# Cosine attention into a leaky-relu MLP on one core: squares and two copies to ScalarE, one weight asked for in a row, two turnings a group later

## The chip, the cores and the metric

The kernel runs on 1 core of one Trainium2 chip. The metric is the device time of one execution in microseconds (us). Engines: TensorE (PE; its weight loads are the row PEld), VectorE (DVE), ScalarE (ACT), GpSimd (POOL) and SyncE (SP). DMAs are asked for on the queues of SP, ScalarE and GpSimd.

## The reference

```python
# q, k, v: (8, 12, 448, 64) f32; tau = 0.1; w_in: (768, 2048); w_out: (2048, 768)
q_n = q / (norm(q, axis=-1) + 1e-6)
k_n = k / (norm(k, axis=-1) + 1e-6)
scores = q_n @ k_n.T / tau
attn = softmax(scores)                    # over the keys
x = (attn @ v).transpose(0, 2, 1, 3).reshape(3584, 768)
h = x @ w_in
out = maximum(0.01 * h, h) @ w_out        # (3584, 768) f32
```

## The kernel before

The twelve heads of a batch are six **pairs** of heads. Pairs are numbered through, `s` from 0 to 47, so that pairs 0 to 5 are batch 0 and 6 to 11 batch 1. The "tenth pair" is `s = 9`. The 448 tokens of a head are three tiles of 128 and a remainder of 64.

What one pair passes through before TensorE can make its scores:

- `load_qk` or `load_pairs`: rows of q and k from DRAM into one of six places in `raw_sb`.
- `squares(s)`, line 173: two multiplications (512 and 384 elements a partition, f32), on GpSimd as a rule; for `nc.scalar` it is an activation with Square.
- `sums(s)`, line 186: two reductions on VectorE.
- `roots(s)`, line 197: Ln and Exp on ScalarE, for the square root.
- `normalise(s)`, line 213: on VectorE an addition (line 217), a reciprocal (218) and two scalings (222) that write `qn`.
- `transposes(s)`, line 248: for `s < 10` seven turnings on TensorE (line 236) into one PSUM bank and a copy into `qkT` (line 260); from 10 on a DMA.

`norm(s)` is roots, normalise, (turnings,) then `hold`, and the squares of a later pair. `hold(x)` (line 511) is a copy of one column on GpSimd: GpSimd's queue goes on only when `x` has been written. All engines run their queues in the order in which the program writes them; nothing reorders them.

Behind the scores stand `key_tiles` (TensorE's scores, ScalarE's Exp into `pe`, or `pr` for the remainders), `totals`, `products` and `scale`, which give `xT`. The MLP of a batch is `firsts` (16 groups m of six matmuls, each drained by ScalarE into `hT` by Prelu, lines 374 to 390) and `groups` or `second` (line 458 or 420, with `w_out_sb`). PSUM has eight banks, given out by age by `banks`.

The stage that the change touches begins at line 754: `attend(NQ - 1)` closes batch 0's attention. Then `firsts(0, ...)` runs batch 0's groups m, and between them, at the m given in a table, the last four pairs that TensorE turns are prepared: pairs 6 to 9. Behind m = 15 the first `visit` starts with `key_tiles([(7, 3), (9, 3)])`, the key remainders of pairs 6 and 7 and of 8 and 9. They need `qkT` of all four. In that stage GpSimd's queue holds, in order: `hold(xT)`, two quarters of `w_out` (line 111, 768 KB each), `hold(qn[6])`, the squares of pair 9, `hold(qn[7])`, a quarter of `w_out`, the squares of pair 10, `hold(qn[8])`, the last quarter, the squares of 11, then loads of v.

Of the kernel before, what the change touches and what calls it, by code (L numbers as in the profile page):

```python
# [16 lines left out]
def kernel(  # L17
# [10 lines left out]
    nc = tc.nc  # L28
# [12 lines left out]
    MT = D_ff // 128  # L41
# [67 lines left out]
    def load_w_out(parts):  # L109
        for m in parts:  # L110
            gp.dma_start(out=w_out_sb[:, m : m + MT // 4], in_=w_out_r[:, m : m + MT // 4])
# [25 lines left out]
    def load_qk(s):  # L137
        if s >= NSLOT:
            return
        b, h0 = s // NPAIR, 2 * (s % NPAIR)  # L140
        both = raw_sb[:, s % NPAIR]
        nc.sync.dma_start(out=both[:, :, 0:3], in_=main(q, b, h0, 2))
        nc.sync.dma_start(out=both[:, :, 4:7], in_=main(k, b, h0, 2))
        for i, x in enumerate((q, k)):
            nc.sync.dma_start(
                out=both[64 * i : 64 * i + 64, :, 3],
                in_=x[b, h0 : h0 + 2, MAIN:S].rearrange("h p d -> p h d"),
            )
        raw[s] = (both[:, :, 0:4], both[:, :, 4:7])
# [23 lines left out]
    def squares(s, engs=(gp, gp)):  # L173
        if s >= NSLOT:
            return
        tiles = []
        for x, eng, name in zip(raw[s], engs, ("sq0", "sq1")):
            sq = sqp.tile(list(x.shape), F32, name=name)
            if eng is nc.scalar:
                nc.scalar.activation(sq, x, func=AF.Square)  # L180
            else:
                eng.tensor_tensor(sq, x, x, op=ALU.mult)  # L182
            tiles.append(sq)
        sqs[s] = tiles

    def sums(s, parts=(0, 1)):
        if s >= NSLOT:
            return
        if s not in ss:
            ss[s] = smp.tile([128, 14], F32, name="ss")  # L190
        for i in parts:
            o = ss[s][:, 0:8] if i == 0 else ss[s][:, 8:14]
            nc.vector.tensor_reduce(  # L193
                o.rearrange("p (h t) -> p h t", h=2), sqs[s][i], axis=AX.X, op=ALU.add
            )

    def roots(s):
        if s >= NSLOT:
            return
        nc.scalar.activation(ss[s], ss[s], func=AF.Ln, bias=tiny)  # L200
        nc.scalar.activation(ss[s], ss[s], func=AF.Exp, scale=0.5)  # L201

    qn, scalings = {}, {}
# [9 lines left out]
    def normalise(s):  # L213
        if s >= NSLOT:
            return
        r = smp.tile([128, 14], F32, name="r")
        nc.vector.tensor_scalar_add(ss[s], ss[s], 1e-6)  # L217
        nc.vector.reciprocal(r, ss[s])  # L218
        qn[s] = qnp.tile([128, 7, 2, D], BF16, name="qn")
        for x, lo, hi, r0 in ((raw[s][0], 0, 4, 0), (raw[s][1], 4, 7, 8)):  # L220
            nt = hi - lo
            scalings[s] = nc.vector.tensor_tensor(  # L222
                qn[s][:, lo:hi],
                x.rearrange("p h t d -> p t h d"),
                r[:, r0 : r0 + 2 * nt].rearrange("p (h t) -> p t h", h=2)
                .unsqueeze(3).to_broadcast([128, nt, 2, D]),
                op=ALU.mult,
            )
# [5 lines left out]
    def one(tp, s, lo, hi):  # L234
        for t in range(lo, hi):
            nc.tensor.matmul(
                out=tp[:, t, :],
                lhsT=qn[s][:, t].rearrange("p h d -> p (h d)"),
                rhs=id128,
                is_transpose=True,  # L240
                start=(t == lo),
                stop=(t == hi - 1),
            )

    def transposed():
        return banks(1).bitcast(BF16)[:, : 7 * 128].rearrange("p (t c) -> p t c", c=128)

    def transposes(s):
        if s >= NSLOT:
            return  # L250
        dst = qtp.tile([128, 7, 128], BF16, name="qkT")
        qkT[s] = dst.rearrange("p t c -> p (t c)")
        if s >= DMA_FROM:
            nc.sync.dma_start(
                out=dst, in_=qn[s].rearrange("p t h d -> p (t h d)"), transpose=True
            )
            return
        tp = transposed()
        one(tp, s, 0, 7)
        nc.vector.tensor_copy(out=dst, in_=tp)  # L260

    pe, pr = {}, {}

# [247 lines left out]
    def hold(x):  # L511
        seen = smp.tile([128, 1], F32, name="seen")
        gp.tensor_copy(out=seen, in_=x)  # L513
# [28 lines left out]
    dst = qtp.tile([128, 7, 128], BF16, name="qkT")  # L542
    qkT[0] = dst.rearrange("p t c -> p (t c)")
    for lo, hi in ((0, 4), (4, 7)):
        tp = transposed()
# [45 lines left out]
    for s in range(2):  # L591
        scores(s, (0, 1))
        fill(2 if s else 5)
        scaled(s)
        scores(s, (2,))
        if s:
            fill(2)
            scores(s, (3,))
        transposes(s + 1)
        fill(2)  # L600
        roots(s + 2)
# [4 lines left out]
    scores(2, (2,))  # L606
    fill(2)
    transposes(3)
    roots(4)
    reciprocals(0)  # L610
# [6 lines left out]
    scores(3, (2,))  # L617
    fill(1)
    transposes(4)
    roots(5)  # L620
    scores(3, (3,))
# [66 lines left out]
    def attend_batch(b):  # L688
        if b == 1:
            load_qk(14)  # L690
            load_qk(15)
            sums(12)
        attend_two(b * NQ)
        if b == 1:
            norm(12)
        attend(b * NQ + 2)


    def norm(s, transposed=True):
        if s >= NSLOT:  # L700
            return
        roots(s)
        normalise(s)
        if transposed:
            transposes(s)
        if s == 10:
            return
        for x in (12, 13) if s == 11 else (s + 4,) if s > 11 else ():
            load_qk(x)
        hold(qn[s][:, 6, 0, 0:1])  # L710
        if s < 9:
            load_w_out((4 * (s - 5),))
        if s == 11:
            squares(12)
        if s != 9:
            squares(s + (3 if s < 9 else 2))

    def firsts(b, begun, between):

        for m in range(begun, AHEAD):  # L720
            pms[b, m] = banks(1, (b, m, 0))
            first(b, m, range(KT - 2))
        for m in range(MT):
            for fn in between.get(m, ()):
                fn()
            first(b, m, range(KT - 2 if m < max(begun, AHEAD) else 0, KT))
# [18 lines left out]
    def at(*steps):  # L745
# [8 lines left out]
    attend(NQ - 1, [lambda m=m: first(0, m, range(KT - 2)) for m in range(3, SOON)])  # L754
    normalise(6)
    hold(xT[0][:, 2 * NQ - 2, 0:1])
    load_w_out((0, 4))
    hold(qn[6][:, 6, 0, 0:1])
    squares(9)
    norm(7, False)  # L760
    sums(8)
    firsts(
        0, SOON, {
            4: [lambda: transposes(6), lambda: norm(8, False)],
            6: [lambda: sums(9)],
            7: [lambda: transposes(7)],
            9: [lambda: norm(9, False)],
            10: [lambda: transposes(8)],
            11: [lambda: sums(10), lambda: load_v(3)],
# [6 lines left out]
    for b in range(B):  # L776
# [26 lines left out]
        s = ready  # L803
# [57 lines left out]
```

## Time and profile before

| what | value |
|---|---|
| runs | 410.40, 408.26, 410.38 us (median 410.38) |
| profiled execution: its own time | 408.75 us |
| profiled execution: span, first to last instruction | 407.0 us |
| granted TensorE clock | 1.0 of full |
| busy share PE, DVE, ACT, POOL | 98%, 47%, 64%, 35% |

A row of a timeline reads: start in us from the span's beginning, duration in us, engine, line, operation, tile written <- tile read, count, and in brackets the idle time before it with what ended it. Rows of equal instructions that follow each other are merged (x4). A row of waits reads: who waited, for whom, us in all, times, the longest. A row of groups ends with busy us, mean ns of one, and idle us.

### The profile page before, as it was taken

What the parts mean: (1) busy time and instruction counts of PE and PEld (TensorE: products, weight loads), DVE (VectorE), ACT (ScalarE), POOL (GpSimd) and SP (SyncE); (2) the same over time, 40 slices, a digit from 0 to 9 for tenths busy, and PEclk for the clock granted to TensorE, in tenths of its full rate; (3) what the DMA queues carried; (4) which work ended last, traced back from release to release, by engine and by line L of the source; (5) the groups of instructions that cost most, each with busy time, mean ns of one, the idle gap of its engine ahead of it and who ended that gap; (6) DMA issues with size and microseconds to landing.
All of it is one profiled execution on the core that took longest, in us unless ns stands there. A gap on an engine that the chain in (4) does not pass through costs nothing.

```text
span 407.0 us, 10163 instructions
## 1 busy us (share of the span) xinstructions
PE 397.6 (98%) x4086; PEld 225.0 (55%) x4096; DVE 191.1 (47%) x405; ACT 262.3 (64%) x454; POOL 143.5 (35%) x218
## 2 busy tenths in 40 slices
PE   7899999999999999999999999999999999999996
PEld 2335655444555655544786555544687555544554
DVE  5987931775674715355463626256262631130021
ACT  4995589566865579645876569845776559844300
POOL 4997632374325414253141622255122500000000
PEclk9999999999999999999999999999999999999999
DMA  7999999599598936588396854685397821110033
GB/s 181 248 224 240 216 180 229 154 177 203 124 199 160 156 72 159 118 131 176 58 183 154 125 128 109 168 117 134 81 168 129 102 46 40 40 41 2 0 78 79
DMA packets 100735, 54.21 MB, mean 133 GB/s; under 512 B 69424, under 2 KB 95440, under 8 KB 100688
## 3 DMA queue, kind: packets, MB, share of 16 engines
q1 hardware_dynamic: 76400, 40.13, 43.3%
q0 software_dynamic: 23440, 12.92, 23.3%
q8 instruction: 32, 0.52, 0.5%
q10 hardware_dynamic: 848, 0.52, 0.4%
q14 instruction: 15, 0.12, 0.1%
HBM read 45.61 MB, written 11.01 MB: 139 GB/s over the span
## 4 chain that ended last, share of the span: by engine, by line
PE 88%; DVE 5%; POOL 3%; DMA 1%; issue 1%; ACT 1%; POOLq 0%
PE ps L383 33%; PE ps L458 31%; PE ps L319 11%; PE ps L279 8%; PE ps L420 5%; DVE qn L222 2%; POOL sq L182 1%; PE ps L306 1%; DMA raw_sb<-in_k_dram 1%; DVE ss L193 1%; POOL v_rem L167 1%; DVE r L218 0%; DVE qkT L260 0%; POOL raw_sb L132 0%; DVE ss L217 0%
## 5 line engine op out<-in xcount | busy, mean ns | idle before, releaser
L383 PE MATMUL ps<-xT,w_in_sb 128*128 128x384 bf16 (+1 forms) x760 | 147.6, 352 | 0.4
L458 PE MATMUL ps<-w_out_sb,hT 64*128 64x384 bf16 x1536 | 144.0, 323 | 0.0
L291 ACT ACTIVATE pe<-ps 128x896 bf16<-128x896 f32 x144 | 124.5, 917 | 17.9 <-PE ps L279 16.0
L383 PEld LDWEIGHTS <-w_in_sb 128*128 128x128 bf16 x768 | 74.1, 98 | 71.7 <-issue 4.0
L390 ACT ACTIVATE hT<-ps 128x384 bf16<-128x384 f32 (+1 forms) x128 | 66.8, 543 | 66.4 <-PE ps L383 65.9
L458 PEld LDWEIGHTS <-hT 64*128 64x128 bf16 x1536 | 84.4, 94 | 44.6 <-PE ps L458 4.2
L182 POOL TENSOR_TENSOR sq<-raw_sb 128x512 f32<-128x512 f32 x92 | 84.9, 944 | 14.8 <-DMA raw_sb<-in_k_dram 13.9
L222 DVE TENSOR_TENSOR qn<-raw_sb,r 128x512 bf16<-128x512 f32 x96 | 59.2, 658 | 1.6
L279 PE MATMUL ps<-qkT 64*128 64x448 bf16 (+1 forms) x384 | 55.0, 353 | 2.1 <-DVE qkT L260 1.6
L193 DVE TENSOR_REDUCE ss<-sq 128x6 f32<-128x384 f32 (+1 forms) x95 | 54.3, 610 | 1.1 <-POOL sq L182 1.1
L470 DVE COPY osb<-ps 128x384 f32<-128x384 f32 x41 | 21.2, 553 | 69.8 <-PE ps L458 38.9
L513 POOL CAST seen<-qn 128x1 f32<-128x1 bf16 x47 | 9.2, 197 | 123.0 <-DVE qn L222 122.5
L217 DVE TENSOR_SCALAR ss<-ss 128x14 f32<-128x14 f32 x48 | 9.8, 205 | 74.0 <-ACT ss L201 73.8
L360 DVE TENSOR_TENSOR xT<-ps,rb 128x448 bf16<-128x448 f32 x48 | 27.8, 620 | 24.6 <-ACT rb L339 24.4
L160 POOL DMA_DIRECT2D v_b<-in_v_dram x24 | 18.6, 778 | 39.9 <-PE ps L319 39.9
L319 PE MATMUL ps<-pe,v_b 128*32 128x448 bf16 x576 | 32.0, 353 | 0.0
L279 PEld LDWEIGHTS <-qkT 64*128 64x128 bf16 (+1 forms) x384 | 17.8, 97 | 18.7 <-issue 7.3
L338 ACT ACTIVATE rb<-ps 128x448 f32<-128x448 f32 x24 | 12.9, 538 | 14.9 <-PE ps L319 13.9
L426 DVE COPY osb<-ps 128x384 f32<-128x384 f32 (+1 forms) x9 | 4.6, 513 | 36.6 <-issue 22.6
L319 PEld LDWEIGHTS <-v_b 128*32 128x32 bf16 x576 | 15.2, 97 | 11.9 <-issue 0.6
L291 ACT ACTIVATE pr<-ps 128x896 bf16<-128x896 f32 x24 | 20.8, 923 | 0.4 <-PE ps L279 0.4
L420 PE MATMUL ps<-w_out_sb,hT 128*128 128x384 bf16 (+1 forms) x144 | 21.0, 308 | 0.0
(50 smaller groups left out, 185.9 us busy)
## 6 DMA issues: line engine op xcount, KB each, us to landing
raw_sb<-in_q_dram SPq DMA_DIRECT2D x46, 192.0 KB, 3.3
raw_sb<-in_k_dram SPq DMA_DIRECT2D x44, 192.0 KB, 3.1
out_dram<-osb SPq DMA_DIRECT2D x30, 192.0 KB, 3.0
v_b<-in_v_dram POOLq DMA_DIRECT2D x24, 192.0 KB, 4.7
out_dram<-osb SPq DMA_DIRECT2D x12, 384.0 KB, 2.7
w_out_sb<-in_moe_w_out_dram POOLq DMA_DIRECT2D x4, 768.0 KB, 13.7
w_in_sb<-in_moe_w_in_dram POOLq DMA_DIRECT2D x3, 512.0 KB, 9.0
w_in_sb<-in_moe_w_in_dram POOLq DMA_DIRECT2D x2, 768.0 KB, 13.7
```

What stands on the lines that cost most here:

```text
L182: eng.tensor_tensor(sq, x, x, op=ALU.mult)
L193: nc.vector.tensor_reduce(o.rearrange("p (h t) -> p h t", h=2), sqs[s][i], axis=AX.X, op=ALU.add)
L222: scalings[s] = nc.vector.tensor_tensor(qn[s][:, lo:hi], x.rearrange("p h t d -> p t h d"), r[:, r0 : r0 + 2 * nt].rearrange("p (h t) -> p ...
L279: nc.tensor.matmul(out=out[:, a, :S], lhsT=x[rows, c0:c1], rhs=x[rows, 0:S], start=True, stop=True,)
L291: nc.scalar.activation(out=dst, in_=sc[:, :, :S], func=AF.Exp, scale=inv_tau)
L319: nc.tensor.matmul(out=x[32 * g : 32 * g + 32, :S], lhsT=weights(g, ki) if ki < 3 else rem(g), rhs=pe[s][:, ki, a, :] if ki < 3 else pr[j] ...
L360: scalings[j, e] = nc.vector.tensor_tensor(xT[m][:, 2 * jj + e, half * S : (half + 1) * S], pos.pop((j, e))[:, :S], rbs[j], op=ALU.mult,)
L383: nc.tensor.matmul(out=pm[:, :n], lhsT=w_in_sb[:, kt, m * 128 : (m + 1) * 128], rhs=xT[c // 2][:, kt, c0 : c0 + n], start=(kt == 0), stop= ...
L390: nc.scalar.activation(out=hT[c][:, m, :n], in_=pms.pop((c, m))[:, :n], func=AF.Prelu, alpha=0.01)
L420: nc.tensor.matmul(out=po2[:, :n], lhsT=hT[c][:, m, ts * 128 : (ts + 1) * 128], rhs=w_out_sb[:, m, lo : lo + n], start=(m == 0), stop=(m = ...
L458: done[p][i] = nc.tensor.matmul(out=pos2[p][:, i, :HALF], lhsT=hT[c][rows, m, ts * 128 : (ts + 1) * 128], rhs=w_out_sb[rows, m, half * HAL ...
L470: copy(out=osb[c, ts][:, half * HALF : (half + 1) * HALF], in_=po2[:, i, :HALF])
```

## The change

Four edits in one stage:

- The squares of pair 9 move from GpSimd, where they stood behind `hold(qn[6])`, to ScalarE, behind roots 7. That `hold` goes.
- The copies of the turned rows of pairs 8 and 9 move from VectorE to ScalarE.
- All four quarters of `w_out` stand behind `hold(xT)` on GpSimd; before, the last two stood behind the holds of pairs 7 and 8.
- The turnings of pair 6 stand ahead of m = 5 instead of m = 4, and those of pair 7 ahead of m = 8 instead of m = 7. `norm(8)` stays at m = 4, so on VectorE it now stands ahead of the copy of pair 6.

```diff
@@ transposes
-        nc.vector.tensor_copy(out=dst, in_=tp)
+        copy = nc.scalar.copy if s > 7 else nc.vector.tensor_copy
+        copy(out=dst, in_=tp)
@@ norm
         hold(qn[s][:, 6, 0, 0:1])
-        if s < 9:
-            load_w_out((4 * (s - 5),))
@@ behind attend(NQ - 1)
     hold(xT[0][:, 2 * NQ - 2, 0:1])
-    load_w_out((0, 4))
-    hold(qn[6][:, 6, 0, 0:1])
-    squares(9)
+    load_w_out(range(0, MT, MT // 4))
     norm(7, False)
+    squares(9, (nc.scalar, nc.scalar))
     sums(8)
     firsts(
         0, SOON, {
-            4: [lambda: transposes(6), lambda: norm(8, False)],
+            4: [lambda: norm(8, False)],
+            5: [lambda: transposes(6)],
             6: [lambda: sums(9)],
-            7: [lambda: transposes(7)],
+            8: [lambda: transposes(7)],
             9: [lambda: norm(9, False)],
             10: [lambda: transposes(8)],
```

## The prediction

> **What bounds the kernel now.** I read the page first: how long, and on which engine the chain that ended last lies.
>
> ```profile
> span 407.0 us, 10163 instructions
> PE 88%; DVE 5%; POOL 3%; DMA 1%; issue 1%; ACT 1%; POOLq 0%
> ```
>
> TensorE holds 88% of the chain and VectorE 5%. The change touches only steps between `attend(NQ - 1)` and the first `visit`, so next I split the span there, with the view that gives the busy time of each engine in each stretch (PE, PEld, DVE, ACT, POOL, granted clock, DMA share, GB/s):
>
> ```profile
> 35.00:52.20 17.20, 16.28 (x124) 9.74 (x120) 16.06 (x33) 8.85 (x24) 12.52 (x18) 1.00 1.14 231
> 52.20:407.00 354.80, 350.70 (x3684) 202.88 (x3692) 148.74 (x314) 225.21 (x382) 103.58 (x156) 1.00 0.62 120
> ```
>
> From 35 to 52.2 VectorE is busy 16.06 of 17.20 us and ScalarE only 8.85; after it VectorE drops to 148.74 of 354.80 and TensorE has 350.70. The first stretch is a VectorE stage, the rest a TensorE stage. So the change can be worth only what TensorE waits in the first stretch. The waits of that stretch name the two that matter, and its timeline gives their place on TensorE:
>
> ```profile
> POOL sq L182 <- DMA raw_sb<-in_k_dram: 2.9, 1, 2.9
> PEld L279 <- DVE qkT L260: 1.1, 1, 1.1
> ```
>
> ```profile
> 37.15 0.77 PE L236 MATMUL ps<-id,qn 128*128 128x128 bf16 x7
> 40.67 0.55 PE L236 MATMUL ps<-id,qn 128*128 128x128 bf16 x7
> 47.30 0.79 PE L236 MATMUL ps<-id,qn 128*128 128x128 bf16 x7
> 47.94 3.09 PE L383 MATMUL ps<-xT,w_in_sb 128*128 128x384 bf16 x18
> 50.95 0.38 PE L279 MATMUL ps<-qkT 64*64 64x448 bf16 x4
> 52.14 0.38 PE L279 MATMUL ps<-qkT 64*64 64x448 bf16 x4 [0.81 <-DVE qkT L260]
> 52.46 1.47 PE L458 MATMUL ps<-w_out_sb,hT 64*128 64x384 bf16 x16
> 53.77 0.35 PE L279 MATMUL ps<-qkT 64*128 64x448 bf16 x2
> 99.28 0.57 PE L279 MATMUL ps<-qkT 64*64 64x448 bf16 x8
> ```
>
> The row at 99.28 is the same two key tiles without a wait: eight in 0.57 us where four take 0.38, so the second four begin 0.19 behind the first. At 50.95 they should have begun at 51.14 and began at 52.14: **1.00 us**. The turnings of pairs 6 and 9 (37.15, 47.30) take 0.77 and 0.79 where an unhindered one takes 0.55: 0.22 and 0.24 more. Together 1.46 us, and that is the most the change can give by this trace.
>
> VectorE, whose last copy releases TensorE at 52.14, and GpSimd beside it:
>
> ```profile
> 36.35 1.16 DVE L222 TENSOR_TENSOR qn<-raw_sb,r 128x512 bf16<-128x512 f32 x2
> 37.91 2.63 DVE L222 TENSOR_TENSOR qn<-raw_sb,r 128x512 bf16<-128x512 f32 x2
> 40.46 1.13 DVE L193 TENSOR_REDUCE ss<-sq 128x8 f32<-128x512 f32 x2
> 42.70 1.16 DVE L222 TENSOR_TENSOR qn<-raw_sb,r 128x512 bf16<-128x512 f32 x2
> 43.78 1.14 DVE L193 TENSOR_REDUCE ss<-sq 128x8 f32<-128x512 f32 x2
> 45.53 0.39 DVE L217 TENSOR_SCALAR ss<-ss 128x14 f32<-128x14 f32 x1
> 46.24 1.46 DVE L222 TENSOR_TENSOR qn<-raw_sb,r 128x512 bf16<-128x512 f32 x2
> 47.63 0.61 DVE L260 COPY qkT<-ps 128x896 bf16<-128x896 bf16 x1
> 48.16 1.13 DVE L193 TENSOR_REDUCE ss<-sq 128x8 f32<-128x512 f32 x2
> 51.47 0.62 DVE L260 COPY qkT<-ps 128x896 bf16<-128x896 bf16 x1
> ```
>
> ```profile
> 35.73 1.57 POOL L111 DMA_DIRECT2D w_out_sb<-in_moe_w_out_dram  x2
> 37.85 2.27 POOL L182 TENSOR_TENSOR sq<-raw_sb 128x512 f32<-128x512 f32 x2
> 41.12 0.82 POOL L111 DMA_DIRECT2D w_out_sb<-in_moe_w_out_dram  x1 [0.27 <-issue]
> 44.86 1.82 POOL L182 TENSOR_TENSOR sq<-raw_sb 128x512 f32<-128x512 f32 x2 [2.92 <-DMA raw_sb<-in_k_dram]
> 47.22 0.81 POOL L111 DMA_DIRECT2D w_out_sb<-in_moe_w_out_dram  x1
> ```
>
> **Part 1: pair 9's squares to ScalarE.** (Pairs are counted from 0: the tenth is 9.) GpSimd's squares at 37.85 ran beside the scalings of pair 7: these took 2.63 us where the rows at 36.35 and 42.70 have 1.16, and the squares 2.27 where 44.86 has 1.82. Without them VectorE gains 2.63 - 1.16 = 1.47. The cost goes to ScalarE, on which these rows bear (line 536 is a square of 512 elements, line 547 the copy of turned rows in two parts, both from the start of the kernel):
>
> ```profile
> 36.37 1.64 ACT L390 ACTIVATE hT<-ps 128x384 bf16<-128x384 f32 x4 [1.16 <-PE ps L383]
> 49.32 0.31 ACT L200 ACTIVATE ss<-ss,tiny 128x14 f32<-128x14 f32 x1 [2.30 <-DVE ss L193]
> 49.78 1.77 ACT L390 ACTIVATE hT<-ps 128x384 bf16<-128x384 f32 x4
> 51.45 0.91 ACT L291 ACTIVATE pr<-ps 128x896 bf16<-128x896 f32 x1
> L536 ACT ACTIVATE sq<-raw_sb 128x512 f32<-128x512 f32 x1 | 0.6, 631 | 0.0
> L547 ACT COPY qkT<-ps 128x512 bf16<-128x512 bf16 x1 | 0.6, 587 | 0.2 <-PE ps L236 0.2
> L547 ACT COPY qkT<-ps 128x384 bf16<-128x384 bf16 x1 | 0.5, 484 | 0.0
> ```
>
> Two squares are at most 2 x 0.63 = 1.26 us against ScalarE's idle 1.16 before 36.37. If pair 9's rows have landed by then it is hidden; GpSimd found them there at 37.85 without a wait, so the latest end is 37.85 + 1.26 = 39.11. Queued behind are the four `hT` of m 0 to 3 (1.64): done between 38.1 and 40.75. TensorE first needs one of these banks for m = 7, and only m 0's (39.5 at the latest); m = 7 begins behind the turning at 40.67, 41.22 now, and without that turning (0.55) and the wait of 0.22 at 40.45. Cost: nothing.
>
> **Part 2: w_out's quarters in a row.** The four are on GpSimd's queue. In the built program the third and fourth first wait for the two halves of w_in that line 107 asked for:
>
> ```profile
> 25.65 1.58 POOL L107 DMA_DIRECT2D w_in_sb<-in_moe_w_in_dram  x2
> DMA to landing us min/median/max: 7.8/10.6/15.2
> ```
>
> The later one, asked at about 26.45, has landed by 26.45 + 15.2 = 41.65. So GpSimd stands until 41.65, issues until 42.5, and is back before pair 10's rows, for which it waits until 44.86 anyway (2.9 us in the waits). Behind it in that queue stand the squares of 10 and 11 and the loads of v; the first start at 44.86 as before. The quarters take 768 KB / 231 GB/s = 3.4 us each and are asked behind pair 10's rows. Cost: nothing, if transfers of one queue land in the order asked (rival B if not).
>
> **Part 3: turnings later and copies moved.** Turning 6 at m = 5 finds its rows (37.51): 0.22 back. VectorE by the spacings of the rows above: scalings 7 end at 37.91 + 1.16 = 39.07; sums 8 begin 0.08 before that, at 38.99 (as 40.46 against 40.54); scalings 8 begin 42.70 - 40.46 = 2.24 later, at 41.23, and end at 42.39; copy 6 takes 0.53 (47.63 to 48.16), so sums 9 begin at 42.84, and norm 9's first step 45.53 - 43.78 = 1.75 later, at 44.59. Its scalings begin about 45.1, **beside** GpSimd's squares of pair 10 from 44.86. By the collision at 37.85 (scalings ended 40.54, 2.69 after the squares began) they end at 44.86 + 2.69 = 47.55, against 47.70 now. So nearly all of the 1.47 is lost again to the same collision one pair later; 0.15 stays. If it costs more than there, they still end no later than now by the row at 46.24, which also waited for these squares: I keep 0 to 0.15.
>
> TensorE goes on behind turning 9 at 47.94 - 0.15 = 47.79, needs 50.95 - 47.94 = 3.01 to the first key tile, 50.80, and asks for the copied rows of pair 9 at 50.80 + 0.19 = **50.99**.
>
> In the kernel before, copy 9 stands on VectorE behind scalings 10 (end 51.55). On ScalarE it stands behind roots 10 and one `hT`. Sums 10 begin at 47.55 - 0.08 = 47.47; roots 10 at +1.16 (48.16 to 49.32), 48.63; `hT` m 12 at +0.46, 49.09; copy 9 at +0.43 (1.77 / 4 less the overlap), 49.52. Its length is not in the trace: between 0.62 (VectorE's) and 0.587 + 0.484 = 1.07 (both parts apart). I take 0.90, the 512 row plus 384 x (0.587 - 0.484)/128, since that row is the same engine, form and source. It ends at **50.42**, 0.57 before TensorE asks; with 1.07, 0.40 before.
>
> The Trainium skill, Perfetto Trace Analysis, section Optimizing Scalar/DVE Operations, says that where VectorE has a faster mode it does such a step faster than ScalarE, and that moving it pays only if VectorE is saturated. The rows bear out both halves: 0.90 against 0.61 makes the two copies 0.58 longer in sum, which by length alone would be lost, but 16.06 of 17.20 busy is saturated.
>
> What is late next: behind copy 9 ScalarE has `hT` m 13 to 15 at 50.4, 50.8, 51.2 (end 51.65) and the first `pr` (0.91, end 52.56). TensorE needs m 15's bank eight matmuls into the row at 52.46, then at 51.31 + 0.65 = 51.96, and the bank of `pr` at 51.31 + 1.31 = 52.62: 0.3 and 0.06 to spare. So the wait moves to the edge and does not come back.
>
> **Sum:** 52.14 - 50.99 = 1.15 us, 1.00 at least. From 52.2 on TensorE has work without a gap, so it reaches the end. The profiled execution took 408.75 (span 407.0 and 1.75 around it): 407.6. But the runs shown are 408.26, 410.38 and 410.40, and the profile is 1.63 below their median; I place the forecast at the mean of all four, 409.45, less 1.15: **408.3**. Own range: 408.26 - 1.15 = 407.1 to 410.40 - 1.00 = 409.4. About 0.5%, 2.05 us, is what a measurement of this kernel can tell from no change, so the forecast is "same".
>
> **Rivals.** *A: more comes off than this trace shows.* The profiled execution is one of the two quick ones. TensorE is gapless at full clock after 52.2, so the 1.63 us by which the median lies higher should sit earlier, perhaps in this VectorE chain, which the change relieves of two copies and a collision. Then 1.15 + 1.63 = 2.78 come off: 410.38 - 2.78 = 407.6. Against it: if slow executions are slow by late rows, TensorE waits for w_in's second half at m = 8 as well (41.65, and m = 8 follows the m = 7 of 40.45 after a third of 3.09 and a turning, at 42.0), and the wait at 51.14 shrinks.
>
> *B: slower, by crowding.* If the transfers of GpSimd's queue share the engines instead of landing in order, the two quarters asked up to 5.6 us earlier (47.22 to 41.65) run ahead of pair 10's rows: up to 2 x 3.4 = 6.8 us of transfer. GpSimd's squares 10, sums 10, roots 10 and with them the `hT` and copy 9 on ScalarE follow. The chain has 1.9 us before anything is lost against now (squares begun at 47.47 - 1.82 = 45.65 still end before sums 10, 0.79 of delay, and 1.15 of gain). At 6.8 the loss is 4.9: 408.75 + 4.9 = 413.6. It makes the kernel slower by over 0.5% from 1.9 + 2.05 = 4.0 us of delay upward. Against it stands how long w_out's own four took to land:
>
> ```profile
> DMA to landing us min/median/max: 12.4/13.7/15.4
> ```
>
> Asked from 35.73 to 47.22, each took about as long as four times its own 3.4: a line served in order, always about as deep.
>
> In the Trainium skill, DMA: Bandwidth & Descriptors, section Queues, rings and completion order, an engine starts the descriptors of one ring in their order and takes turns only between queues; by that rule B can't be, since all these transfers are GpSimd's.
>
> *C: it doesn't do what it says.* Copy 9 is still behind roots 10, hence behind the same chain. If ScalarE runs 1.7 us later than worked out (0.57 + 1.15), its copy comes when VectorE's did: 408.75, no change. For it: ScalarE's idle 2.30 before 49.32 is all wait for sums 10.
>
> **How the numbers follow.** Forecast 0.40, C 0.07: both "same", 0.47. A 0.36: "faster", high because two of four executions shown are 2 us slower than the profiled one and their cause is not in the trace. B 0.17: "slower". The range leaves out B alone: low is the quickest run shown less all of TensorE's waits, 408.26 - 1.46 = 406.8; high the slowest run with C and 0.2 for a wait on `pr`, 410.6.
>
> **What would show it.** Right: the second key tile 0.19 behind the first; scalings 7 in 1.16; scalings 9 in some 2.5, beside squares 10; squares 10 still at 44.86; ScalarE's copy 9 about 0.9 long and ending before 51. Wrong: squares 10 later than 46 (B), TensorE waiting for `hT` or `pr` from 51 to 53 (the edge was mis-sized), or a second key tile released by ScalarE (C).

## The result, and the profile after

| kernel | executions | median us | lowest to highest | profiled execution, its span |
|---|---|---|---|---|
| before | 6 | 410.33 | 408.26 to 410.68 | 408.75, 407.0 |
| after | 6 | 407.12 | 406.90 to 407.20 | 407.09, 405.3 |

The changed kernel takes 0.9926 of the time of before, 95% interval [0.9907, 0.9946]: 0.74% or 3.2 us less. Two things are to be explained: the gain is nearly three times the 1.15 us that was worked out, and the spread has gone with it. Executions of before lie 2.4 us apart, those of after 0.3.

The first lines are the page's span and chain by engine, then the stretches of the stage and of what follows (columns: PE, PEld, DVE, ACT, POOL busy, granted clock, DMA share, GB/s).

```profile
span 405.3 us, 10173 instructions
PE 93%; POOL 3%; DVE 1%; DMA 1%; issue 1%; ACT 0%; POOLq 0%
```

```profile
35.00:50.50 15.50, 15.49 (x117) 9.69 (x118) 13.83 (x32) 10.37 (x26) 10.54 (x16) 1.00 1.13 235
50.50:405.30 354.80, 351.15 (x3696) 202.68 (x3688) 147.30 (x313) 226.12 (x383) 102.83 (x155) 1.00 0.60 121
```

The stage ends at 50.5 instead of 52.2, and TensorE is busy 15.49 of its 15.50 us. What follows lasts 354.80 us as before. VectorE's share of the chain has gone from 5% to 1%. TensorE's timeline in the stage:

```profile
37.90 0.55 PE L236 MATMUL ps<-id,qn 128*128 128x128 bf16 x7
41.22 0.55 PE L236 MATMUL ps<-id,qn 128*128 128x128 bf16 x7
43.56 0.55 PE L236 MATMUL ps<-id,qn 128*128 128x128 bf16 x7
46.87 0.55 PE L236 MATMUL ps<-id,qn 128*128 128x128 bf16 x7
47.27 3.09 PE L384 MATMUL ps<-xT,w_in_sb 128*128 128x384 bf16 x18
50.28 0.57 PE L280 MATMUL ps<-qkT 64*64 64x448 bf16 x8
50.79 1.47 PE L459 MATMUL ps<-w_out_sb,hT 64*128 64x384 bf16 x16
```

All four turnings take the unhindered 0.55, the two key tiles are one row of eight in 0.57, and no row carries a wait. All 1.46 us of waits that the trace of before showed are gone. The lines are one higher than before from line 261 on. VectorE, GpSimd and ScalarE, each from its timeline:

```profile
37.69 1.16 DVE L222 TENSOR_TENSOR qn<-raw_sb,r 128x512 bf16<-128x512 f32 x2
44.37 0.19 DVE L217 TENSOR_SCALAR ss<-ss 128x14 f32<-128x14 f32 x1
44.87 1.47 DVE L222 TENSOR_TENSOR qn<-raw_sb,r 128x512 bf16<-128x512 f32 x2
46.26 1.13 DVE L193 TENSOR_REDUCE ss<-sq 128x8 f32<-128x512 f32 x2
```

```profile
40.69 0.74 POOL L111 DMA_DIRECT2D w_out_sb<-in_moe_w_out_dram  x1 [2.88 <-DMA w_in_sb<-in_moe_w_in_dram]
43.49 1.82 POOL L182 TENSOR_TENSOR sq<-raw_sb 128x512 f32<-128x512 f32 x2 [1.76 <-DMA raw_sb<-in_k_dram]
45.87 2.15 POOL L182 TENSOR_TENSOR sq<-raw_sb 128x512 f32<-128x512 f32 x2
```

```profile
35.00 1.04 ACT L180 ACTIVATE sq<-raw_sb 128x512 f32<-128x512 f32 x2
48.25 0.90 ACT L261 COPY qkT<-ps 128x896 bf16<-128x896 bf16 x1
50.39 0.49 ACT L391 ACTIVATE hT<-ps 128x384 bf16<-128x384 f32 x1 [0.47 <-PE ps L384]
```

Scalings 7 (37.69) take 1.16 instead of 2.63. Squares 9 on ScalarE end at 36.04, ahead of the first `hT` (36.15). Squares 10 start at 43.49, not at 44.86, and meet scalings 9 (44.87) only with their tail: 1.47. Squares 11 (45.87) begin while scalings 9 still run, and here it is GpSimd that takes longer, 2.15 instead of 1.82. Copy 9 on ScalarE ends at 49.15, 1.32 before TensorE asks (50.28 + 0.19 = 50.47).

### The profile page after: what moved, and what is told of

The parts are those of the page before. It is cut to its first block, busy times and chain, and to the rows that moved or that the text cites. A ratio compares the mean times of both kernels' runs of the same rounds, so it can differ in the third digit from the quotient of the medians.

```text
span 405.3 us, 10173 instructions
## 1 busy us (share of the span) xinstructions
PE 398.5 (98%) x4096; PEld 225.0 (56%) x4096; DVE 187.7 (46%) x403; ACT 265.0 (65%) x458; POOL 140.7 (35%) x215
## 4 chain that ended last, share of the span: by engine, by line
PE 93%; POOL 3%; DVE 1%; DMA 1%; issue 1%; ACT 0%; POOLq 0%
PE ps L384 36%; PE ps L459 31%; PE ps L320 11%; PE ps L280 8%; PE ps L421 5%; POOL sq L182 1%; PE ps L307 1%; DMA raw_sb<-in_k_dram 1%; POOL v_rem L167 1%; DVE qn L222 1%; PE ps L236 1%; POOL raw_sb L132 0%; POOL v_b L160 0%; POOL seen L514 0%; DVE qkT L261 0%
## 5 line engine op out<-in xcount | busy, mean ns | idle before, releaser
L182 POOL TENSOR_TENSOR sq<-raw_sb 128x512 f32<-128x512 f32 x90 | 82.4, 937 | 12.5 <-DMA raw_sb<-in_k_dram 11.9
L222 DVE TENSOR_TENSOR qn<-raw_sb,r 128x512 bf16<-128x512 f32 x96 | 56.6, 631 | 2.0 <-DMA raw_sb<-in_q_dram 0.3
```

The lines of the kernel that those rows point to most:

```text
L222: scalings[s] = nc.vector.tensor_tensor(qn[s][:, lo:hi], x.rearrange("p h t d -> p t h d"), r[:, r0 : r0 + 2 * nt].rearrange("p (h t) -> p ...
```

## The experiments

Edits are against the kernel before unless the text says against the kernel after. The spread of before was the first question, so a second trace of it was taken. Over all the comparisons its 82 executions lie between 408.0 and 411.7, of which 23 are under 409.2 and the others at 409.9 or more; its median was 410.43, 409.95 and 410.40 in the three groups of experiments below.

### Each part alone

**The squares alone**

```diff
     hold(qn[6][:, 6, 0, 0:1])
-    squares(9)
     norm(7, False)
+    squares(9, (nc.scalar, nc.scalar))
```

> Only pair 9's squares move to ScalarE (behind norm 7); copies, quarters and turnings stay as before. Theory 1 (chain): all of the gain is TensorE's waits in this stage, set by VectorE's chain, and the executions of before at 410.4 have longer waits there. Then scalings 7 take 1.16 instead of 2.63, TensorE still waits at the second key tile for VectorE's copy 9, by 0 to 0.9 us less than before: 0.2 to 1.1 us faster than an equal execution of before. Theory 2 (elsewhere): the 2 us between the executions of before come from outside the stage, and this kernel's executions spread over 2 us just the same. Theory 3 (port): the collision of squares 9 with scalings 7 alone makes the slow executions; then all executions here gather in the low group, near 408.

Measured: 407.5 us (407.19 to 407.76), ratio 0.9922 [0.9909, 0.9935]. One part has nearly the whole gain, and the spread is gone with it. None of the three theories had all of this: the third had one level, but near 408, and the first a wait left at the second key tile. VectorE, GpSimd and TensorE in its profiled execution:

```profile
45.13 1.41 DVE L222 TENSOR_TENSOR qn<-raw_sb,r 128x512 bf16<-128x512 f32 x2
46.89 1.83 POOL L182 TENSOR_TENSOR sq<-raw_sb 128x512 f32<-128x512 f32 x2
50.97 0.57 PE L279 MATMUL ps<-qkT 64*64 64x448 bf16 x8
```

Scalings 9 begin before squares 10 have ended (45.52) and are done before squares 11 begin. No wait is left at the second key tile, though copy 9 is still on VectorE: it ends at 50.91, 0.25 before TensorE asks. From the first matmul of m = 0 (35.27) to there (51.16) it takes 15.89 us.

**The copies alone**

```diff
-        nc.vector.tensor_copy(out=dst, in_=tp)
+        copy = nc.scalar.copy if s > 7 else nc.vector.tensor_copy
+        copy(out=dst, in_=tp)
```

> Only the copies of pairs 8 and 9 move to ScalarE. Theory 1: copy 9 no longer stands behind scalings 10, ends about 50.6, and the wait of 1.00 us at the second key tile goes: 1.0 us off (407.8 in the profiled state of before), 2 to 3 off the median of before; scalings 7 still 2.63. Theory 2: 1.0 off each execution, spread of 2 us stays. Theory 3 (port): the slow executions stay slow, since the collision of squares 9 with scalings 7 stays; median about 1 us under that of before.

Measured: 409.45 us (408.88 to 411.15), ratio 0.9981 [0.9969, 0.9994]: by the medians 1.0 less, about the wait of 1.00 at the second key tile, and a spread of 2.3 stays. The 2 to 3 us of the first theory did not come. The profiled execution is the slowest of the twelve, 411.15; VectorE and TensorE in it:

```profile
46.22 3.30 DVE L222 TENSOR_TENSOR qn<-raw_sb,r 128x512 bf16<-128x512 f32 x2
```

```profile
48.48 0.40 PE L236 MATMUL ps<-id,qn 128*128 128x128 bf16 x4 [1.47 <-DVE qn L222]
49.58 0.50 PE L236 MATMUL ps<-id,qn 128*128 128x128 bf16 x3 [0.70 <-DVE qn L222]
49.87 4.52 PE L384 MATMUL ps<-xT,w_in_sb 128*128 128x384 bf16 x18
54.32 0.57 PE L280 MATMUL ps<-qkT 64*64 64x448 bf16 x8
```

The key tiles no longer wait (eight in 0.57), but turning 9 waits twice, 1.47 and 0.70, for scalings 9, which take 3.30, and the eighteen matmuls behind it take 4.52 us instead of 3.09. The trace on which the prediction was built has no such wait. How many of the twelve executions have it is not seen.

**The turnings alone**

```diff
-            4: [lambda: transposes(6), lambda: norm(8, False)],
+            4: [lambda: norm(8, False)],
+            5: [lambda: transposes(6)],
...
-            7: [lambda: transposes(7)],
+            8: [lambda: transposes(7)],
```

> Only turnings 6 and 7 a group later. Theory 1: TensorE's 0.22 at turning 6 goes, and comes back at the second key tile, for VectorE's chain is as long as before: no change (within 0.2 us), with the executions spread as those of before. Theories 2 and 3: the same spread of 2 us too. A gain of over 1 us would speak against all three.

Measured: 410.38 us (410.02 to 411.74), ratio 1.0005 [0.9992, 1.0018]: nothing by itself, as expected.

**The kernel before, a second trace**

> The kernel before once more, for a second trace. Theory 1: if this execution is near 410.4, its second key tile waits some 2 us longer than the 1.00 of the first trace, or TensorE waits at m = 8 or at turning 9; if near 408.5 it looks like the first. Theory 2: an execution near 410.4 shows the extra time ahead of 33 us.

Measured: 410.17 us, span 408.4. This trace shows an execution of the usual level. GpSimd, VectorE and TensorE in it:

```profile
43.66 1.82 POOL L182 TENSOR_TENSOR sq<-raw_sb 128x512 f32<-128x512 f32 x2 [1.91 <-DMA raw_sb<-in_k_dram]
45.56 0.81 POOL L111 DMA_DIRECT2D w_out_sb<-in_moe_w_out_dram  x1
46.39 2.31 POOL L182 TENSOR_TENSOR sq<-raw_sb 128x512 f32<-128x512 f32 x2
```

```profile
45.83 3.29 DVE L222 TENSOR_TENSOR qn<-raw_sb,r 128x512 bf16<-128x512 f32 x2
```

```profile
48.08 0.40 PE L236 MATMUL ps<-id,qn 128*128 128x128 bf16 x4 [0.79 <-DVE qn L222]
49.18 0.34 PE L236 MATMUL ps<-id,qn 128*128 128x128 bf16 x3 [0.70 <-DVE qn L222]
53.56 0.38 PE L279 MATMUL ps<-qkT 64*64 64x448 bf16 x4 [0.81 <-DVE qkT L260]
```

Pair 10's last rows land 1.2 us **earlier** than in the first trace (43.43, 44.63 there): squares 10 begin at 43.66 instead of 44.86. Squares 11 follow at 46.39, fall on scalings 9, and these take 3.29 instead of 1.46. From the first matmul of m = 0 (34.83; 35.02 in the first trace) to the second key tile (53.56; 52.14) this execution takes 18.73 us where the first took 17.12: 1.61 more. What is left behind the second key tile is 354.8 us in both, and in after. So the theory for the rest of the study: **GpSimd's squares and VectorE's scalings hold each other up whole instructions long, and in most executions of before a second such meeting, squares 11 with scalings 9, costs another 1.6 us.** By this theory it is early data that takes them to the upper level.

### The order of squares and scalings

**Squares 11 held back**

```diff
@@ norm
-        if s != 9:
-            squares(s + (3 if s < 9 else 2))
+        if s != 8:
+            squares(s + (3 if s < 8 else 2))
```

> The kernel before, with one edit: GpSimd's squares of the twelfth pair (index 11) wait for the scalings of pair 9 instead of those of pair 8, so they cannot run beside the scalings of pair 9; squares 9 stay on GpSimd and still meet scalings 7. Theory (what makes most executions of before take 410.4 is that squares 11 come early, behind early rows, and hold up scalings 9 and with them turning 9 for some 1.9 us): about 408.4, with scalings 9 at 1.2 to 1.5 us, no wait over 0.3 at turning 9, scalings 7 still near 2.6, the 1.0 us wait at the second key tile still there or a little less, and executions that agree within a microsecond. Rival (the collision of squares 9 with scalings 7 alone is what costs, by the lateness that it hands on): no change, 410.2 to 410.5. Rival (squares 11 later make the sums and scalings of pair 11 late): 411 or more.

Measured: 408.32 us (407.85 to 408.50), ratio 0.9965 [0.9944, 0.9986]. GpSimd, VectorE and TensorE:

```profile
47.55 1.82 POOL L182 TENSOR_TENSOR sq<-raw_sb 128x512 f32<-128x512 f32 x2
```

```profile
37.51 2.62 DVE L222 TENSOR_TENSOR qn<-raw_sb,r 128x512 bf16<-128x512 f32 x2
46.11 1.16 DVE L222 TENSOR_TENSOR qn<-raw_sb,r 128x512 bf16<-128x512 f32 x2
```

```profile
51.71 0.38 PE L279 MATMUL ps<-qkT 64*64 64x448 bf16 x4 [0.80 <-DVE qkT L260]
```

As the theory has it: the spread falls from over 3 us to 0.65, the time goes to the lower level of before, scalings 9 take 1.16, and the 1.00 at the second key tile is still there. So the second meeting makes the difference between the two levels of before.

**Squares 9 on GpSimd, but later**

```diff
@@ norm
         hold(qn[s][:, 6, 0, 0:1])
+        if s == 7:
+            squares(9)
@@ behind attend(NQ - 1)
-    hold(qn[6][:, 6, 0, 0:1])
-    squares(9)
     norm(7, False)
```

> The kernel before, with one edit: the squares of the tenth pair (index 9) stay on GpSimd but wait for the scalings of pair 7 instead of those of pair 6; ScalarE gets nothing. Theory (it is the meeting of squares 9 with scalings 7 that costs, not the engine): scalings 7 at 1.2, scalings 8 and 9 earlier by about 1.4, scalings 9 ahead of squares 11, and a time near that of the squares' move to ScalarE alone, 407.4 to 407.9. Rival (ScalarE's taking over of the work is the gain, since GpSimd then has less in its line): squares 10 and 11 come as late as before or later by some of the 1.8 us, a collision moves to scalings 8 or 9, and the time is 409 to 410.4.

Measured: 408.04 us (407.50 to 408.49), ratio 0.9970 [0.9950, 0.9990]. GpSimd and VectorE:

```profile
39.69 1.82 POOL L182 TENSOR_TENSOR sq<-raw_sb 128x512 f32<-128x512 f32 x2
```

```profile
38.19 1.16 DVE L222 TENSOR_TENSOR qn<-raw_sb,r 128x512 bf16<-128x512 f32 x2
```

ScalarE gets nothing here, and 1.9 us of before's 409.95 come off all the same. The median is 0.14 above the band expected. It is 0.5 above that of the squares on ScalarE, but in another group of runs, and the stage of the two traces differs by 0.2 only, so how much better a place ScalarE is stays open. Most of the gain is that squares 9 and scalings 7 no longer meet, and that scalings 9 (45.47) with that come ahead of squares 11 (47.29).

**Rows that come later**

```diff
         if s == 4:
+            load_w_out((0,))
             for part in range(2):
...
-    load_w_out((0, 4))
+    load_w_out((4,))
```

> The kernel before, with one edit: the first quarter of w_out is asked for ahead of the rows of pairs 10 and 11 instead of behind them, so that these rows land some 3 us later (about 46.5 to 48 instead of 43.4 to 44.6). Theory (early rows let squares 11 fall on scalings 9): squares 10 start near 47 and squares 11 near 49, behind scalings 9, which take 1.2 to 1.5; turning 9 does not wait; what stays is the wait of about 1 us at the second key tile, or up to 1.8 if copy 9 or sums 10 come later; the time is 408.5 to 409.5, less than the 410.4 of before although its data come later. Rival (late data cost: sums, scalings and turning of pairs 10 and 11 come late in the next stage): 411.5 to 413.5.

Measured: 413.33 us (410.79 to 414.98), ratio 1.0088 [1.0053, 1.0123]. The expectation was wrong in the total; the time is in the band of its rival, by another path. Squares 10 did move to 47.61 and scalings 9 did take 1.16, but:

```profile
53.78 0.59 PE L279 MATMUL ps<-qkT 64*64 64x448 bf16 x4 [3.05 <-DVE qkT L260]
```

Copy 9 stands on VectorE behind sums 10 and scalings 10, which wait for squares 10. So before has a window. Of the landings that were traced in it, 43.4 brings squares 11 onto scalings 9, 44.6 does not, and at 47.4, here, the second key tile begins 3.24 us late (53.78 against 50.35 + 0.19) instead of 1.00.

**All but the squares** (against the kernel after)

```diff
+    hold(qn[6][:, 6, 0, 0:1])
+    squares(9)
     norm(7, False)
-    squares(9, (nc.scalar, nc.scalar))
```

> The changed kernel without the move of the squares: squares 9 are on GpSimd again behind the scalings of pair 6; the two copies on ScalarE, the quarters in a row and the later turnings stay. Theory: scalings 7 take 2.6 beside squares 9 again, scalings 8 and 9 are late by about 1.4, squares 11 fall on scalings 9 or on the small operations ahead of them, turning 9 waits 1 to 2 us, and no wait is left at the second key tile since copy 9 is on ScalarE: 409.2 to 409.8, within 0.4 of the copies alone (409.45). Rival (the copies, quarters and turnings together give the gain without the squares): 407.1 to 407.6.

Measured: 409.17 us (408.50 to 411.62), ratio 0.9998 [0.9975, 1.0022]. The median is as expected, but by this interval it can't be told from before, and the way was another:

```profile
41.92 1.82 POOL L182 TENSOR_TENSOR sq<-raw_sb 128x512 f32<-128x512 f32 x2
43.83 1.81 POOL L182 TENSOR_TENSOR sq<-raw_sb 128x512 f32<-128x512 f32 x2
45.73 1.81 POOL L182 TENSOR_TENSOR sq<-raw_sb 128x512 f32<-128x512 f32 x2
```

```profile
48.16 0.81 PE L236 MATMUL ps<-id,qn 128*128 128x128 bf16 x7 [1.38 <-DVE qn L222]
```

GpSimd stands for w_in's half, so squares 9 come at 41.92 and miss scalings 7 (1.16 there). Then the three pairs of squares follow each other without a gap, and the third falls on scalings 9; turning 9 waits 1.38.

### Quarters and copies

**The quarters alone**

```diff
-        if s < 9:
-            load_w_out((4 * (s - 5),))
...
-    load_w_out((0, 4))
+    load_w_out(range(0, MT, MT // 4))
```

> The kernel before, with the quarters of w_out in a row alone. The run without the squares' move showed what the row of quarters does to GpSimd's line: it stands until the half of w_in has landed, so squares 9 start near 41.9 instead of 37.5, too late to meet scalings 7. Theory (only the order of GpSimd's squares against VectorE's scalings decides): scalings 7 at 1.2, squares 9, 10 and 11 in one run from 41.9 to 47.5, scalings 9 at 2.0 to 2.6 beside squares 11, a wait of some 1.2 to 1.7 at turning 9 and the 1.0 at the second key tile, since copy 9 is still on VectorE: 409.2 to 410.2. Rival (asking for the quarters at once is a gain of its own): 408.0 to 408.5.

Measured: 409.74 us (408.23 to 410.82), ratio 0.9988 [0.9969, 1.0008]. The meeting moves from scalings 7 (1.16 in its trace) to scalings 9 (2.43), and what that is worth can't be told from nothing. The time and the way are those of the theory.

**All but the copies** (against after; line 260 is VectorE's copy again)

> The changed kernel with copies 8 and 9 back on VectorE; squares on ScalarE, quarters in a row, later turnings stay. Theory (the squares' move makes scalings 9 so early that copy 9 is in time on VectorE too): 407.0 to 407.6, no wait over 0.3 at the second key tile, and copy 9 beginning on VectorE near 47 to 50. Rival (copy 9 still stands behind scalings 10 and ends too late): the 1.0 us wait is back, 408.0 to 408.3.

Measured: 408.02 us (407.66 to 408.76), ratio 0.9945 [0.9925, 0.9964]. The rival was right: copy 9 is late again. The profiled execution is the slowest of the six, 408.76. GpSimd, VectorE and TensorE in it:

```profile
45.03 2.27 POOL L182 TENSOR_TENSOR sq<-raw_sb 128x512 f32<-128x512 f32 x2
```

```profile
44.32 0.65 DVE L217 TENSOR_SCALAR ss<-ss 128x14 f32<-128x14 f32 x1
45.28 2.42 DVE L222 TENSOR_TENSOR qn<-raw_sb,r 128x512 bf16<-128x512 f32 x2
```

```profile
47.76 0.34 PE L236 MATMUL ps<-id,qn 128*128 128x128 bf16 x3 [0.68 <-DVE qn L222]
52.15 0.38 PE L279 MATMUL ps<-qkT 64*64 64x448 bf16 x4 [0.81 <-DVE qkT L260]
```

Up to scalings 9 the queues of VectorE and GpSimd are those of after. But pair 10's last rows landed 0.4 us earlier (42.89, 43.27 in after): norm 9's first step (line 217) came into the second multiplication of squares 10 and took 0.65 instead of 0.19, and squares 11, at 45.03, were ahead of scalings 9. So the wait of 0.68 at turning 9 comes with the landing, not with the copies. What the copies' move takes away is the 1.00 at the second key tile (52.15 against 50.96 + 0.19), where copy 9 on VectorE stands behind scalings 10. By the medians that move is worth 0.9 us here (408.02 against 407.12); what the other five executions met is not seen.

**All but the quarters** (against after; the loads behind the holds are back)

> The changed kernel with the quarters of w_out asked for one behind each of the scalings, as before. Theory (the quarters' places matter only through the order of GpSimd's squares, and squares 9 are not in its line any more): 407.0 to 407.6. If the DMA issue between squares 10 and 11 lets squares 11 fall on scalings 9 at their start, up to 1 us more, 408.2. Rival (the row of quarters carries part of the gain by itself): 408 to 408.5 without such a meeting.

Measured: 407.11 us (406.95 to 407.32), ratio 0.9924 [0.9906, 0.9942], profiled span 405.3: the same as after. Beside the other parts the row of quarters gives and costs nothing.

**Rows that come later, in the kernel after**

```diff
         if s == 4:
+            load_w_out((0,))
...
-    load_w_out(range(0, MT, MT // 4))
+    load_w_out(range(MT // 4, MT, MT // 4))
```

> The changed kernel with the first quarter of w_out asked for ahead of the rows of pairs 10 and 11, as in the run of the kernel before that came out at 413.3 with a wait of 3.05 us at the second key tile (copy 9 stood on VectorE behind sums 10 and scalings 10, which waited for squares 10). Theory (with copy 9 on ScalarE the key tiles no longer depend on those rows): squares 10 near 47, no wait over 0.3 at the second key tile, 407.1 to 408.7, the upper end if the 1.5 us that the later stages lost with the late rows are lost again. Rival (late rows cost the same wherever the copy is done): 411 to 413.5.

Measured: 409.08 us (408.42 to 411.55), ratio 0.9985 [0.9966, 1.0004]. Neither expectation: late rows cost 2.0 us here (409.08 - 407.12) and 3.4 before (413.33 - 409.95). TensorE and ScalarE, in an execution of 410.73:

```profile
52.35 0.38 PE L280 MATMUL ps<-qkT 64*64 64x448 bf16 x4 [1.75 <-ACT qkT L261]
```

```profile
50.57 0.31 ACT L200 ACTIVATE ss<-ss,tiny 128x14 f32<-128x14 f32 x1 [4.05 <-DVE ss L193]
51.40 0.90 ACT L261 COPY qkT<-ps 128x896 bf16<-128x896 bf16 x1
```

Copy 9 on ScalarE is still behind roots 10 and so behind pair 10's rows. It ends at 52.30, 3.15 later than in after, of which 1.32 were to spare: 1.83 by that reckoning; the second key tile begins 1.94 late (52.35 against 50.22 + 0.19). That is about the 2.0 us of the medians. This execution lost 1.7 more behind the second key tile (356.6 us instead of 354.8), where the granted clock was 0.50 from 54 to 56 us. The copies' move buys slack, not independence.

## Why the prediction was right or wrong

The time (407.12) lies in the range, below the likeliest value (408.3), and the outcome is the one that rival A had: faster by over 0.5%. That the range holds it is in part luck: its low end, 406.8, took all of TensorE's waits off the quickest execution shown, and the larger gain came by a second meeting that the text did not know of.

**What bounds the kernel: right.** All of the gain is in the stage named: 17.12 and 18.73 us in the two traces of before, 15.68 in after (34.79 to 50.47), with 354.8 behind it each time. And 18.73 - 15.68 = 3.05 is, but for 0.16, the difference of the medians.

**Squares to ScalarE: right, and too small.** They are hidden (end 36.04; 39.11 was the bound), and scalings 7 fall to 1.16. The step that failed is the next one, "nearly all of the 1.47 is lost again to the same collision one pair later; 0.15 stays". VectorE's chain came out as worked out: norm 9's first step was put at 44.59 and began at 44.37, and the stage begins 0.23 earlier in after. What was wrong is squares 10, put at 44.86. They began at 43.49 in after, at 43.66 in before's second trace and by 44.12 in all the experiments but the two that make the rows late: the rows of the first trace were the late ones. Scalings 9 then met only the tail of squares 10 (1.47, not about 2.5), sums 10 began at 46.26 instead of 47.47, and the whole 1.46 came off instead of 1.15.

**The forecast's point: wrong by its placing.** The profiled execution was one of the rarer ones without the second meeting. 1.15 was taken off a mean of 409.45, as if the 1.63 between the levels would stay.

**Rival A: the sum was near (407.6), the mechanism only half.** It said that the extra time sits in VectorE's chain in this stage; it does, as squares 11 on scalings 9. Moving squares 9 makes scalings 9 early enough to be ahead of squares 11, so it takes away both: the first meeting is gone, and squares 11 come behind. What the text said against A, that the longer executions come "by late rows", was the wrong way round. One trace of before could not tell this; a second one did.

**What decides the second meeting.** The traces sort by one thing: where norm 9's first step (line 217) falls against the two multiplications of squares 10, of which the first takes 1.03. In five traces (before's first, after, the squares alone, squares 9 later, all but the quarters) the step begins 0.49 to 0.88 us after squares 10; scalings 9 then begin before squares 10 have ended and take 1.41 to 1.47. In six (before's second, the copies, the turnings and the quarters alone, all but the squares, all but the copies) it begins 1.01 to 2.07 us after them, squares 11 get ahead, and scalings 9 take 2.42 to 3.30, or with the turnings alone the step itself takes 1.78. With squares 11 held back it begins 1.19 after them, and scalings 9 take 1.16. After, at 0.88, is only 0.13 from the nearest of the six. So its narrow spread may hang on when pair 10's rows land; no run made them land earlier in after itself.

**The Trainium skill on the port.** SBUF — State Buffer, section Who interferes with whom, says that a VectorE instruction with two SBUF inputs contends with a GpSimd instruction that reads SBUF, that the port pair they share is an exclusive lock, and that issue order decides who is blocked. The traces agree in the main: scalings take 1.16 alone and 2.4 to 3.3 where squares come first, while sums, which that section exempts, take 1.13 beside squares 11 in after. Which of the two comes first moved the time by 1.6 us here. The order of the records does not always tell it (last section), and no run here tests the port apart from anything else that the two engines may share.

**Quarters: right.** GpSimd stood until 40.69 (41.65 was the bound) and was back before pair 10's rows; without the quarters' move the time is the same (407.11). The issue between squares 10 and 11, which goes with it, was no protection against the second meeting: in before's second trace and with the copies alone it stood there, and scalings 9 took 3.29 and 3.30.

**Copies: right in their length, not in their share.** Copy 9 took 0.90 as worked out, and the edge behind it (`hT` of m 15, `pr`) did not become a wait. But the sum took the 1.00 at the second key tile off by the copies' move, and the squares' move alone takes it off too.

**Turnings: right.** They give at most the 0.21 of turning 6 (0.76 in the trace of the squares alone, 0.55 in after), and alone nothing.

**Rival B: no sign of it.** Pair 10's rows landed earlier in after than in the first trace of before (43.27, 44.63), not later. And one quarter asked ahead of them made them land at 47.37 in before, 2.7 to 3.9 us later than in its two traces, about the 3.4 that a quarter was reckoned at: nothing here speaks against a line served in order. **Rival C** did not happen, but its mechanism is real: with squares 10 4.6 us later (48.13) TensorE waited 1.75 for ScalarE's copy.

**Open:** what makes pair 10's rows land at 43.4 in one execution of before and at 44.6 in another. Only two executions of before were seen in a trace.

## What to carry to other kernels

Where the executions of one kernel lie at two levels, read a trace of each before working out a sum: the difference may be a wait that the change also removes. GpSimd's squares and VectorE's scalings behaved here as one resource with an order. Where a kernel has such a pair, list which of the instructions can meet when data come early and when they come late, and move the one that is free to go elsewhere, or later. A gap in a queue, such as a DMA issue, is not enough to keep two others apart.

## What the hardware showed that was not expected

**TensorE's clock fell to half after short waits.** In the trace of the copies alone (columns as above, the seventh being the granted clock):

```profile
46.00:48.00 2.00, 1.01 (x7) 0.39 (x4) 1.97 (x2) 0.99 (x3) 1.98 (x4) 1.00 1.15 209
48.00:50.00 2.00, 0.82 (x8) 0.65 (x9) 2.00 (x3) 0.00 (x0) 1.28 (x2) 0.84 1.16 210
50.00:52.00 2.00, 2.00 (x8) 0.93 (x7) 1.31 (x5) 1.36 (x4) 1.90 (x3) 0.50 1.17 212
```

Waits of 1.47 and 0.70 us, with half the time idle over 4 us, were followed by a clock of 0.50, and eighteen matmuls took 4.52 us instead of 3.09: 1.43 more on top of the waits. In before's second trace, with waits of 0.79 and 0.70, the clock stayed at 1.00. With before's rows made late, the wait of 3.05 was followed by 0.50 from 54 to 56 us, and 356.3 us instead of 354.8 lay behind the second key tile: part of why late rows cost so much. A single wait of 1.75 us, in after with late rows, was followed by 0.50 too; one of 1.64, with the turnings alone, was not (1.00 throughout). What decides between them is not shown. The Trainium skill, TensorE: Matmul & The Clock Gate, section What's actually happening, puts the drop behind an idle window of about 3.4 us; here no single wait was that long.

**A scaling is held before the squares are recorded.** In before's second trace scalings 9 begin at 45.83, while GpSimd is in a DMA issue (45.56 to 46.37) and squares 11 are recorded only from 46.39. Alone, the first of the two takes 0.69 and would be done by 46.52; it ended at 48.02, and TensorE got its rows at 48.08. With the turnings alone the small step ahead of the scalings (line 217) took 1.78 instead of 0.17, from 45.81, though squares 11 are recorded only from 46.47:

```profile
45.81 1.78 DVE L217 TENSOR_SCALAR ss<-ss 128x14 f32<-128x14 f32 x1
```

An issue with no squares behind it did not do this: with squares 11 held back, scalings 9 began at 46.11 beside the issue of 45.84 to 46.65 and took 1.16. Why VectorE should be held before the squares are recorded was not tried.
